# One PSUM tile for each bank of the two MoE stages, and the state product on all four quarters of TensorE

## Chip, cores and metric

One core of a Trainium2 chip runs the whole program. The metric is the device time of one execution in microseconds, the median of three runs: 1067.89 us for the kernel before (1065.71 to 1068.6).

## The reference

Gated linear attention is followed by two mixture layers without routing ("moe" and "moe2"), all in float32. The sizes are 4 batches x 8 heads x 768 positions x 48 per head, 3072 tokens of 384, and hidden widths of 1536 and 768.

```
f = sigmoid(f_logit)
for t in range(768):
    state = f[:, :, t, :, None] * state + outer(k[:, :, t], v[:, :, t])
    y[:, :, t] = q[:, :, t] @ state
x = y as (3072, 384)
x = ((x @ w_a) * (x @ w_b)) @ w_out
out = max(x @ w1, x @ w2, x @ w3) @ w_out2
```

## The kernel before

**Segments.** The tokens are cut into 12 segments of 256, three to a batch. A segment goes through attention and then through the first moe; its result is stored to a scratch in DRAM. When all 12 are done, the second moe runs over 6 blocks of 512 tokens.

**Attention of a segment** (`attn_steps`, line 384; `direct_steps`, 311, or `near_steps`, 218, ahead of it). Products inside groups of 8 positions are made on VectorE and GpSimd. TensorE turns the decayed k, q and the partial result (`p_tr`, `p_od`), then makes the products between positions (`p_sc`, 491, and `p_av`, 508, with the masks of line 505 between them) and carries the state: `p_u` (452) makes the new part of the state of each of four chunks of 64 positions, `decay` (462) and `gain` (466) add it up in `st`, and `p_in` (479) multiplies the state that a chunk begins with by that chunk's decayed q, which line 547 puts into `kt`. Heads lie in eight places: `hl`, the half of the 128 partitions (0 to 63 or 64 to 127), and `hi` from 0 to 3. `p_in` issues 64 products of 48 x 48 by 48 x 64 in a segment (48 where the state is still zero). It reads partitions `64 * hl` and writes PSUM partitions `64 * hl`. `p_av` reads the half `hl ^ hp` and writes the half `hl`, with both values of `hp` next to each other.

**First moe of a segment** (`moe1_steps`, 571). Numbers are split into a high and a low part, so each product is three matmuls in place of one. For each pair jj of the 12 tiles of hidden width: `up` a twice (9 matmuls of 256 columns each, line 591), a copy `c_a` on ScalarE out of PSUM (597), `up` b twice, `v_ab` on VectorE (601) that multiplies a by the b in PSUM, `c_g` on ScalarE (605) and `v_g` on VectorE (610) that split the product, and two `y` (9 matmuls each, 619) that add onto the three sums of the result. `c_y` (625, 627) copies the finished sums out.

**Second moe.** `up2` (777) writes tiles of one bank each, from the pool `ps_p` of four buffers, which ScalarE (787) and VectorE (789) read; `down` (804) adds onto four sums of 384 columns, which `c_down` (811) copies out.

**PSUM.** The pool `ps_m` holds one tile of four banks, made once (line 138), and everything of the two moes but `up2` lives in it: a in bank 0, b in bank 1, the sums of `y` in banks 2 and 3, and the four sums of `down` in banks 0 to 3. The conversion of the first three weight groups on TensorE (`s5p`, 698, and one copy of 3 x 384 columns, `s5c`, 706) uses banks 0 to 2. The other four banks are attention's (`ps_o`, `ps_w`) and later `up2`'s.

```
bank = ps_m.tile([P, 4, 2 * SEG], F32, name="bank")
pair = [bank[:, i].rearrange("p (a x) -> p a x", a=2) for i in range(4)]
ps2[w] = pair["ab".index(w)]           # up
yps[0], yps[1] = pair[2], pair[3][:, 0] # y
o_ps[t] = bank[:, t, 0:DM]             # down
```

**Order.** Every piece of work is a step with a letter for its kind (`step`, 146). `ORDER` is a string written out ahead of time: its letters say which kind's next step is issued, so it sets the order in which each engine's instructions, and the DMAs of SyncE's queue, are queued; the semaphores between engines are placed by the tile framework from what each instruction reads and writes. `flex` steps (150) may run on VectorE or GpSimd; `ON_POOL` lists the numbers of those that run on GpSimd.

Of the kernel before, what the change touches and what calls it, by code (L numbers as in the profile page):

```python
# [19 lines left out]
    "zzzqkjillvtrdrcrzrdrdTUddrTdrUdrddrdTdUrdr0dPdPrdkb1brg20PrPqhgq31gr2b5jbg3grgghbggr0hrgPhrhb1r6Thrb"  # L20
    "52Vrrcd3rTdT0rVrdTr61Pr25hrrh3hkhh6Phv4h0tPhP01P2h31P4Tlbl2Uxb0ddxdTdUd13d2TssUe4s3ed0edm4md0m1d2mnd"
    "PP3m1jbbfgmg2nmg3hgmfcg4Pnybgfg0gyhgdmgv4mbn1mbhm2PPbf3ThdybnhVm4mdThTyVhTdfPrdnrrmrhfrmrhndthmdhfmd"
    "hn0hmdPfhdn10Pd2yhy13PdP2cyh43yPdmlb4cmxfbnmdfxmdnmddyfsdkydneqjPPbfmbgdyhgdPgybdgdcmgdbmngdbnmnhYgd"
    "mgdfhmnmfhmnghyfgdyndmfmdyndvydmdmdPfPndmbhmbPfhnmtdhdhyhydhdmhdhPfdhndPfmhdydPcdPdcyhdPdmlbmxnddmdx"
    "PPfbdmbjnmhqkgdsmmfcdyendygfdPnmgdbgfmbdbygdgydhgdmnngnmYhmfnhmfmgnhdmygfvdnmfmdmdnmdPfPdmbhbmPdmhtd"
    "mhdhyhdhynhPdhfPdndyhfydnPfPdyhdcydcdPmlbdbmxddmndxPPdbgmbjmhqkgfgsPgdnmbgemcdbmfbdnygfyhndyfdmgdgyd"
    "gdhymndnmYnhmdmhvmfdnmfmgnddyfdnPPfybdbydPhdytmdmdhmndhmdhmdfmdnfmdnhcydhcdyhdhPdhPddmkhdmfqjdnPPfmh"
    "ydncdPylbddbdmxddPPbdxmbgdmhfgPdnmbgvfmsgdnybgebygdmghmfggnhmgmfhydhPdPybhbmnnnYPdfhmtdhnmfhdmnyhdhd"
    "hyhPdhdPdmhdPfPdnmdcfchmdyndPdylbdmxdddPPbgkmbgxgggmhfgndPqjmbhsmfbeynbgdygchmmfgdnmhfmhngdydydmddmf"
    "dnmfmdndyvdydmdPfPndmbfmbdhPdytyhdmhnndhnmYhmdhfhnPdhdPfmhdyndydccdPdPmhdPdmlbddkdqbmxPPfbdmbjxnmghd"  # L30
    "gfPdnmbgdysgfdbygcdgmbenhmgdmgdfmgndyfghynmdmhvfmhnydydmdmfdnPfPdmbhbyndPhdythdmhdhmhdhmhdPhdfndPfmh"
    "dydccdydPnndPnYdmhkmddPfqdjnmlbmbfxdmnmxcdmfdnmdPsPfdmbnbemdPgfdmbdbhmgbdmgdmdvyydydnyfgndPfgmdnmfmg"
    "ndhmgdmfmdgmdmgdhyyghPdnhybdbyfhdnPfmtndmfcdhmcdhhdmhdyydydkhydhqdhjPnnnYhdfPnmhdcPfPdmhdmnddmdddmfn"
    "mdmfvdnPmlbddmxfdPPbgxybdgmdghdmsmgdgdygePdnPbfybdnybhmdfggmgdngyfdnmhcmdhmcfhmddmmdydPnkdydbfbjyqhd"
    "nyfmdnmcfmdmddPdyhtdhdyhdhydhPndnnYfmdvnmfmhndmhdmfdnmfmdnmdmfdmmdmdddPyhdydydnfPdnPdfmdhmdmmPylbbyx"
    "nfynxyfnmfmsmnemyfynfyyyPPnbmdcbgdmgnghYPnggPdbgdmcbmbghmdfnmfmgndyghymdghdPmbhdbmfhnPfmthndyhhydhhm"
    "dhhdPhdfnPfmdhydydPPmhPnmlbbmxPPfbgxmbgggnmghgfPhPnbyggsgygbebmhmhPfmbhhnmbPfmhnhhyhhhyhhPPmhmfnmfmy"
    "ymnnnYPfmnfmmnmmfnmfmnmmfmmmyyynfPnyhfmnmfmnmmfmmmPybyxynxfynyfnyfsywWeWyWWmWnWnWmWWmWnmWAWmfWmnBpAf"
    "mCyWDyBWCnmWEDmfWnmWfAmWEWyWynBGYCmGAmHfmHGBmDHCmpnufDEunfnEAmfyyGBAHyCyNuGBDMCGuEDuMAEHuNHNBpMuCMDM"
    "uNENuMMuMummnmmfnmfmnoyyWWmWufnfoyAyunBnYCoooNoNMoDMoMoEoNoNouMoMooouuMNMuNoMooouuMGGHNHGMuNHpuMuMNM"  # L40
    "uNuMoMoOuOXuXuuooOoOXoNoNMoMuMXNNMuMuMuuuoooooNoNMoMuMuuGGHGHHoopNoNMoMoMooNoNMouoMoOoOXoOuOXuMNMuXN"
    "uMXuMNMuNuMuMuuuoooooNoNMoMuMuuooNoNMoMuMuuGGHGHHoopNoNMoMoMooNoNMouoMoOoOXoOuOXuMNMuXNoMoXoouuMNMuN"
    "oMooouuMNMuNuMuMNMuNuMuMuuoGoGHoGHoHoNoNMoMoMooNoMouoNoOoOXoOuOXuMuXMNMuNXoMooouuMNMuNoMooouuMNMuNoM"
    "ooouuMNMuNoMooouuMNMuNoMooouuMNMuNoMoOoOXoOuOXuMNMuXNuMXoMoNouMuNuMuMuuuooNoNMoMuMuuooNoNMoMuMuooNoN"
# [952 lines left out]
```

## Time and profile before

| what | value |
|---|---|
| median of three runs | 1067.89 us |
| the profiled execution, its own time | 1064.77 us |
| its span, first to last instruction | 1063.0 us |
| mean granted TensorE clock | 0.990 of full speed |
| first matmul of the first moe | 60 us |
| first matmul of the second moe | 726.6 us |
| last `up` of the first moe | 762 us |

The span is what the trace shows; 1.8 us lie around it. The trace has three parts: the start with loads and conversions of weights and the attention of segment 0 (to 60 us), the 12 segments of the first moe with the other segments' attention between them (60 to some 762 us, the second moe's first products among the last of them), and the second moe. TensorE is the engine that is busy throughout, so the reading goes by what ends its idle times. A matmul's row is longer than the distance to the next one, since matmuls are pipelined: distances between starts tell the pace, durations do not.

### The profile page before, as it was taken

The page shows a single profiled execution, that of the slowest core. Times are in us where ns is not written, and L with a number is a line of the kernel's source. Part 1 is how long each engine was busy: PE and PEld are TensorE (multiplying, and loading weights), DVE is VectorE, ACT ScalarE, POOL GpSimd, SP SyncE. Part 2 cuts the span into 40 slices and gives each one's busy share as a digit, 9 for nine tenths or more (in the row PEclk, how much of TensorE's full clock was granted, in tenths as well). Part 3 has the DMA queues.
Part 4 walks back from the last instruction along what each step waited for, and adds up shares of the span by engine and source line. Part 5 has one row for each costly group of instructions (what it writes and reads, how often), then busy time and mean ns, then how long its engine had stood idle before and what let it go on. Part 6 is the DMA issues. An engine that isn't in the chain of part 4 may idle for free.

```text
span 1063.0 us, 23346 instructions
## 1 busy us (share of the span) xinstructions
PE 944.6 (89%) x10367; PEld 851.2 (80%) x10367; DVE 508.2 (48%) x714; ACT 330.3 (31%) x504; POOL 324.5 (31%) x299
## 2 busy tenths in 40 slices
...
DMA packets 31973, 72.93 MB, mean 69 GB/s; under 512 B 4224, under 2 KB 13184, under 8 KB 31872
## 3 DMA queue, kind: packets, MB, share of 16 engines
...
## 4 chain that ended last, share of the span: by engine, by line
PE 80%; DVE 7%; ACT 6%; issue 2%; DMA 1%; SPq 0%; DVEq 0%; ACTq 0%
PE bank L591 29%; PE p L777 21%; PE bank L619 15%; PE bank L804 7%; DVE a L601 4%; ACT a L597 3%; PE o L517 1%; PE o L487 1%; PE w L500 1%; PE w L397 1%; DVE gl L610 1%; PE w L459 1%; PE o L397 1%; ACT ub L811 1%; DMA xf<-xf 1%
## 5 line engine op out<-in xcount | busy, mean ns | idle before, releaser
L591 PE MATMUL bank<-xh,ua 128*128 128x256 f32 x864 | 169.2, 293 | 34.6 <-DVE a L601 29.5
L619 PE MATMUL bank<-gh,uo 128*128 128x256 f32 x864 | 165.5, 290 | 22.3 <-ACT a L597 14.4
L591 PE MATMUL bank<-xh,ub 128*128 128x256 f32 x864 | 165.1, 288 | 20.6 <-ACT a L597 17.6
L591 PEld LDWEIGHTS bank<-xh,ua 128*128 128x128 f32 x864 | 135.5, 193 | 45.3 <-DVE a L601 38.4
L777 PE MATMUL p<-ub,u 128*128 128x512 f32 x486 | 165.5, 395 | 0.0
L619 PEld LDWEIGHTS bank<-gh,uo 128*128 128x128 f32 x864 | 134.3, 192 | 30.4 <-ACT a L597 19.0
L591 PEld LDWEIGHTS bank<-xh,ub 128*128 128x128 f32 x864 | 134.2, 192 | 27.4 <-ACT a L597 22.5
L601 DVE TENSOR_TENSOR a<-a,bank 128x512 f32<-128x512 f32 x72 | 49.5, 687 | 200.9 <-PE bank L591 153.5
L591 PE MATMUL bank<-xl,ua 128*128 128x256 f32 x432 | 123.1, 285 | 0.6 <-DVE xl L582 0.6
L619 PE MATMUL bank<-gl,uo 128*128 128x256 f32 x432 | 122.6, 284 | 0.1
L591 PE MATMUL bank<-xl,ub 128*128 128x256 f32 x432 | 121.9, 282 | 0.0
L605 ACT CAST gh<-a 128x512 fp32r<-128x512 f32 x72 | 44.7, 620 | 218.0 <-DVE a L601 169.8
L777 PEld LDWEIGHTS p<-ub,u 128*128 128x128 f32 x486 | 90.7, 187 | 20.5
L789 DVE TENSOR_TENSOR ua<-ua,p 128x512 f32<-128x512 f32 x72 | 49.4, 686 | 112.5 <-PE p L777 111.8
L777 PE MATMUL p<-ua,u 128*128 128x512 f32 x324 | 101.7, 395 | 0.0
L610 DVE TENSOR_TENSOR gl<-a,gh 128x512 fp32r<-128x512 f32 x72 | 61.0, 847 | 51.9 <-ACT gh L605 51.7
L591 PEld LDWEIGHTS bank<-xl,ua 128*128 128x128 f32 x432 | 83.5, 193 | 0.9 <-DVE xl L582 0.9
L619 PEld LDWEIGHTS bank<-gl,uo 128*128 128x128 f32 x432 | 83.0, 192 | 0.3 <-DVE gl L610 0.3
L597 ACT COPY a<-bank 128x512 f32<-128x512 f32 x72 | 42.3, 587 | 131.6 <-PE bank L591 92.9
L591 PEld LDWEIGHTS bank<-xl,ub 128*128 128x128 f32 x432 | 82.7, 191 | 0.0
L777 PEld LDWEIGHTS p<-ua,u 128*128 128x128 f32 x324 | 60.6, 187 | 13.8
L793 ACT CAST uo<-ua 128x512 fp32r<-128x512 f32 x36 | 22.3, 620 | 150.4 <-DVE ua L789 88.1
...
## 6 DMA issues: line engine op xcount, KB each, us to landing
...
```

Source lines behind the costliest of these rows:

```text
L397: mm(pair[0][h], lhsT=pair[1][h], rhs=ident[half(h), half(h)], is_transpose=True, start=first_of_bank(n), stop=True, skip_group_check=True)
L459: mm(ws["u"][half(hl), par, g, hi], lhsT=k64n[ps, g, hi, half(hl)], rhs=vst[ps, g, hl ^ (hi // 2), hi], start=True, stop=True, skip_group_ ...
L591: mm(ps, lhsT=col(w, i, j, h), rhs=x2[x][:, i], start=(n == 0), stop=(n == 3 * KC - 1), skip_group_check=True)
L597: act.copy(out=g2[jj][0], in_=ps2["a"])
L601: vec.tensor_mul(out=a, in0=a, in1=ps2["b"])
L605: act.copy(out=g2[jj][1], in_=g2[jj][0])
L610: vec.tensor_sub(out=g2[jj][2], in0=a, in1=gh.bitcast(F32))
L619: mm(ps, lhsT=wts["o", j // 3][:, j % 3, w, m * P:m * P + P], rhs=g, start=(j == j0 and n == 0 and m != 1), stop=(j == j1 - 1 and n == 2), ...
L777: mm(ps, lhsT=col(n, i, f, w), rhs=y[:, i], start=(c == 0), stop=(c == 3 * KC - 1))
L789: vec.tensor_max(out=hset[k][0], in0=hset[k][0], in1=u_ps[b, f, n])
L793: act.copy(out=hh, in_=h)
L804: mm(o_ps[t], lhsT=h[:, t * P:t * P + P], rhs=wts["q", f // 3][:, f % 3, w], start=(f == 0 and n == 0), stop=(f == NF - 1 and n == 2))
```

## The change

- The tile of four banks is gone. Each use asks the pool for a tile of one bank by name: `pa` and `pb` for `up`, `y01` and `y2` for `y`, the four in turn for `down`, and `pa`, `pb`, `y01` for `s5p`, which is now three steps, each with its own copy `s5c` of 384 columns.
- For the heads with `hi` of 2 and 3 the state lies in the other half of the partitions: `p_u` writes it there, line 547's product of q is made by three instructions (one for `hi` 0 and 1 on all partitions, two for `hi` 2 and 3, each reading one half of the partitions and writing the other), and so is `tot`, the decay over a chunk (line 422). `p_in` then reads the half `hl ^ (hi // 2)`, and its loop goes over `hi` in the order 0, 2, 1, 3.
- `ORDER` and `ON_POOL` are new as a whole: 2583 steps in place of 2523 (48 from the split products, 12 from `s5p` and `s5c`), 639 of them flex in place of 591. Which steps there are is otherwise the same.

```diff
--- before.py
+++ after.py
@@ -17,51 +17,52 @@
 
 
 ORDER = (
...
 )
 
 
 ON_POOL = {
...
 }
 
 NEAR = 2
@@ -135,8 +136,8 @@
     ps_o = at_stack.enter_context(tc.tile_pool(name="ps_o", bufs=1, space=bass.MemoryType.PSUM))
     ps_w = at_stack.enter_context(tc.tile_pool(name="ps_w", bufs=1, space=bass.MemoryType.PSUM))
 
-    bank = ps_m.tile([P, 4, 2 * SEG], F32, name="bank")
-    pair = [bank[:, i].rearrange("p (a x) -> p a x", a=2) for i in range(4)]
+    def bank(tag):
+        return ps_m.tile([P, 2 * SEG], F32, tag=tag, name=tag)
 
     raw = {}
     wts = {}
@@ -376,6 +377,8 @@
         flex("d", lambda e: e.tensor_add(out=opv[:, :, 4:8, 0:D], in0=opv[:, :, 4:8, 0:D],
                                    in1=pv[:, :, 0, :].rearrange("p (h t) d -> p h t d", h=2)))
 
+    CROSS = ((slice(0, 2), slice(0, P), slice(0, P)), (slice(2, 4), slice(0, 64), slice(64, P)),
+             (slice(2, 4), slice(64, P), slice(0, 64)))
     xf = {}
     KL = [k8.rearrange("p x r -> p (x r)"), k16.rearrange("p x l r -> p (x l r)"), k32.rearrange("p x l r -> p (x l r)")]
     q8 = qt.rearrange("p (x two) r -> p two x r", two=2)[:, 1]
@@ -419,7 +422,10 @@
             flex("g", lambda e: e.tensor_mul(out=a4, in0=fv[:, :, :, 3], in1=tv[:, :, :, 3]))
             flex("g", lambda e: e.tensor_mul(out=gt[:, :, 4:8], in0=gt[:, :, 0:4], in1=_bc(a4[:, :, 1], 2, 4)))
             flex("g", lambda e: e.tensor_mul(out=ft[:, :, 4:8], in0=ft[:, :, 8:12], in1=_bc(a4[:, :, 0], 2, 4)))
-            flex("g", lambda e: e.tensor_mul(out=tot.rearrange("p a b -> p (a b)"), in0=a4[:, :, 0], in1=a4[:, :, 1]))
+            a4v = a4.rearrange("p (a b) i -> p a b i", a=4)
+            for a, dst, src in CROSS:
+                flex("g", lambda e, a=a, dst=dst, src=src: e.tensor_mul(
+                    out=tot[dst, a], in0=a4v[src, a, :, 0], in1=a4v[src, a, :, 1]))
 
         def p_tr(src):
             w = ws["x"] = banks(ps_w, "w")
@@ -456,7 +462,7 @@
                     for par in range(2):
                         for hl in range(2):
                             ps = half(par)
-                            mm(ws["u"][half(hl), par, g, hi], lhsT=k64n[ps, g, hi, half(hl)],
+                            mm(ws["u"][half(hl ^ (hi // 2)), par, g, hi], lhsT=k64n[ps, g, hi, half(hl)],
                                rhs=vst[ps, g, hl ^ (hi // 2), hi], start=True, stop=True, skip_group_check=True)
 
         def decay(c, e):
@@ -481,12 +487,13 @@
             for c in range(4):
                 if first and c == 0:
                     continue
-                for hi in range(4):
+                for hi in (0, 2, 1, 3):
                     o = (hi % 2) * SEG + 64 * c
                     for hl in range(2):
+                        r0 = 64 * (hl ^ (hi // 2))
                         mm(os_[0][64 * hl:64 * hl + D, hi // 2, o:o + 64],
-                           lhsT=st[64 * hl:64 * hl + D, c, hi * D:hi * D + D],
-                           rhs=qv[64 * hl:64 * hl + D, hi, c], start=False, stop=True, skip_group_check=True)
+                           lhsT=st[r0:r0 + D, c, hi * D:hi * D + D],
+                           rhs=qv[r0:r0 + D, hi, c], start=False, stop=True, skip_group_check=True)
 
         def p_sc(g):
             w = ws["s", g] = banks(ps_w, "w").rearrange("p h (i x) -> p h i x", i=2)
@@ -544,7 +551,10 @@
         step("b", lambda: act.copy(out=q16[:, :, 0, :], in_=sib(qt)[:, :, 1, 0, :]))
         flex("h", lambda e: e.tensor_mul(out=q16[:, :, 1, :], in0=sib(qt)[:, :, 1, 1, :], in1=_bc(tsib[:, :, 2], 2, 8)))
         flex("h", lambda e: e.tensor_mul(out=q32, in0=hc(qt)[:, :, 4:8, :], in1=_bc(ft[:, :, 8:12], 3, 8)))
-        flex("h", lambda e: e.tensor_mul(out=hc(kt), in0=hc(qt), in1=_bc(ft[:, :, 0:8], 3, 8)))
+        for a, dst, src in CROSS:
+            y = slice(4 * a.start, 4 * a.stop)
+            flex("h", lambda e, y=y, dst=dst, src=src: e.tensor_mul(
+                out=hc(kt)[dst, y], in0=hc(qt)[src, y], in1=_bc(ft[src, y, 0:8], 3, 8)))
         if late:
             late(os_)
         step("P", p_u)
@@ -583,7 +593,7 @@
 
         def up(w, j):
             if j % 2 == 0:
-                ps2[w] = pair["ab".index(w)]
+                ps2[w] = bank("p" + w).rearrange("p (a x) -> p a x", a=2)
             ps = ps2[w][:, j % 2]
             n = 0
             for i in range(KC):
@@ -611,7 +621,8 @@
 
         def y(j, j0, j1):
             if j == j0:
-                yps[0], yps[1] = pair[2], pair[3][:, 0]
+                yps[0] = bank("y01").rearrange("p (a x) -> p a x", a=2)
+                yps[1] = bank("y2")[:, 0:SEG]
             gh, gl = (g[:, j % 2] for g in g2[j // 2][1:])
             for m in range(KC):
                 ps = yps[0][:, m] if m < 2 else yps[1]
@@ -695,17 +706,14 @@
             w = wts[groups[n]]
             e.tensor_sub(out=w[:, :, 1], in0=t, in1=w[:, :, 0].bitcast(F32))
 
-        def s5p(n):
+        def s5p(n, i):
             t = live[n][1].bitcast(F32).rearrange("p (i c) -> p i c", i=3)
-            w = wts[groups[n]]
-            for i in range(3):
-                mm(bank[:, i, 0:DM], lhsT=ident, rhs=t[:, i], start=True, stop=False, skip_group_check=True)
-            for i in range(3):
-                mm(bank[:, i, 0:DM], lhsT=minus, rhs=w[:, i, 0], start=False, stop=True, skip_group_check=True)
-
-        def s5c(n):
-            live.pop(n)
-            act.copy(out=wts[groups[n]][:, :, 1], in_=bank[:, 0:3, 0:DM])
+            ps = live[n, i] = bank(("pa", "pb", "y01")[i])[:, 0:DM]
+            mm(ps, lhsT=ident, rhs=t[:, i], start=True, stop=False)
+            mm(ps, lhsT=minus, rhs=wts[groups[n]][:, i, 0], start=False, stop=True)
+
+        def s5c(n, i):
+            act.copy(out=wts[groups[n]][:, i, 1], in_=live[n, i])
 
         for n in range(len(groups)):
             step(kinds[0], s1, n)
@@ -713,8 +721,9 @@
             flex(kinds[2], lambda e, n=n: s3(n, e))
             step(kinds[3], s4, n)
             if n < on_pe:
-                step(kinds[5], s5p, n)
-                step(kinds[6], s5c, n)
+                for i in range(3):
+                    step(kinds[5], s5p, n, i)
+                    step(kinds[6], s5c, n, i)
             else:
                 flex(kinds[4], lambda e, n=n: s5(n, e))
 
@@ -799,7 +808,7 @@
     def down(b, f, t):
         _, hh, hl = hset[(b * NF + f) % 2]
         if f == 0:
-            o_ps[t] = bank[:, t, 0:DM]
+            o_ps[t] = bank(("pa", "pb", "y01", "y2")[t])[:, 0:DM]
         for n, (h, w) in enumerate(((hh, 0), (hh, 1), (hl, 0))):
             mm(o_ps[t], lhsT=h[:, t * P:t * P + P], rhs=wts["q", f // 3][:, f % 3, w], start=(f == 0 and n == 0), stop=(f == NF - 1 and n == 2))
 
```

## Rows read from the trace of the kernel before

**Rows 1.** The page, part 1: busy time, share of the span, instructions of each engine.

```profile
PE 944.6 (89%) x10367; PEld 851.2 (80%) x10367; DVE 508.2 (48%) x714; ACT 330.3 (31%) x504; POOL 324.5 (31%) x299
```

**Rows 2.** Waits of PE: waited for, us in total, times, longest us.

```profile
PE bank L591 <- DVE a L601: 30.3, 39, 1.3
PE bank L591 <- ACT a L597: 19.7, 28, 1.4
PE bank L619 <- ACT a L597: 14.4, 21, 0.8
PE bank L619 <- DVE a L601: 7.6, 9, 0.9
PE bank L804 <- ACT ub L811: 6.8, 12, 0.6
PE bank L591 <- ACT ysb L627: 3.2, 3, 1.3
```

**Rows 3.** Timeline, 653 to 659 us: start us, us, engine, what, [idle before].

```profile
653.68 0.28 PE L591 MATMUL bank<-xl,ua 128*128 128x256 f32 x1
654.76 0.28 PE L591 MATMUL bank<-xl,ub 128*128 128x256 f32 x1
655.07 0.58 ACT L597 COPY a<-bank 128x512 f32<-128x512 f32 x1 [2.93 <-PE bank L591]
655.71 0.50 PE L591 MATMUL bank<-xh,ub 128*128 128x256 f32 x2 [0.68 <-ACT a L597]
...
658.98 0.50 PE L591 MATMUL bank<-xh,ua 128*128 128x256 f32 x2 [0.85 <-DVE a L601]
```

**Rows 4.** Chain in order of time, 640 to 690 us: start us, us, what.

```profile
646.15 2.16 PE bank L619 x18
...
655.71 2.43 PE bank L591 x18
...
658.98 2.42 PE bank L591 x18
...
662.06 2.43 PE bank L591 x18
```

**Rows 5.** Groups by form: count, busy us, mean ns, idle before and what ended it.

```profile
L777 PE MATMUL p<-ub,u 128*128 128x512 f32 x486 | 165.5, 395 | 0.0
...
L610 DVE TENSOR_TENSOR gl<-a,gh 128x512 fp32r<-128x512 f32 x72 | 61.0, 847 | 51.9 <-ACT gh L605 51.7
...
L601 DVE TENSOR_TENSOR a<-a,bank 128x512 f32<-128x512 f32 x72 | 49.5, 687 | 200.9 <-PE bank L591 153.5 <-PE bank L619 33.9 <-ACT a L597 13.5
...
L605 ACT CAST gh<-a 128x512 fp32r<-128x512 f32 x72 | 44.7, 620 | 218.0 <-DVE a L601 169.8 <-PE bank L619 48.3
...
L811 ACT COPY ub<-bank 128x384 f32<-128x384 f32 x24 | 10.9, 480 | 35.3 <-PE bank L804 35.3
```

**Rows 6.** Timeline of PE, one p_in and one p_av of a segment.

```profile
477.47 1.94 PE L487 MATMUL o<-kt,st 48*48 48x64 f32 x62
...
481.35 0.89 PE L517 MATMUL o<-ab,vlev 64*48 64x64 f32 x48
```

**Rows 7.** Groups by form: products into kt (1024 columns) and k32 (512).

```profile
L547 POOL TENSOR_TENSOR kt<-qt,ft 128x1024 f32<-128x1024 f32 x8 | 18.3, 2285 | 20.5 <-PE w L397 16.5 <-DVE a L601 3.9
...
L540 DVE TENSOR_TENSOR k<-kt,gt 128x512 f32<-128x512 f32 x8 | 5.8, 724 | 0.1
...
L547 DVE TENSOR_TENSOR kt<-qt,ft 128x1024 f32<-128x1024 f32 x4 | 5.7, 1424 | 0.0
...
L540 POOL TENSOR_TENSOR k<-kt,gt 128x512 f32<-128x512 f32 x4 | 5.6, 1392 | 0.2
```

**Rows 8.** Stretches: length, busy us of PE, PEld, DVE, ACT, POOL; clock.

```profile
80.00:140.00 60.00, 50.44 (x868) 46.56 (x866) 44.41 (x58) 23.40 (x33) 31.47 (x24) 1.00 0.26 89
140.00:560.00 420.00, 375.19 (x5326) 352.51 (x5326) 245.24 (x356) 116.73 (x196) 215.34 (x202) 1.00 0.18 58
```

**Rows 9.** Line 708: duration ns min/median/max, start.

```profile
L708 ACT CAST ua<-bank x1: 1141/1141/1141, 28.5 to 28.5; 128x1152 fp32r<-128x1152 f32 x1
```

More of the change, by code (lines that the diff above doesn't have):

```diff
@@ L19 @@
 ORDER = (
[L20 to L44, printed above, removed]
@@ L45 @@
-    "MoMoMooNoMoooOoOXoOOXXX"
+    "zzzqkjtivllrdrcdrzrdrTrUdddrTdUdrddTrdUdrdPdPbr0gdjkggb1vg02PrPhrggh3gr1gbr52b5rg6gb5gr3gh6r505rhhPr"
+    "hbr61Tbkh65Vcq26T0qTrhrV63r1T2rPr5h5rh6h3h5hrd6P0hrdr4hdPt610h2PP13h4PTlblU2xb0ddxdTd3d1Ud4sTssUded0"
+    "ededm2PPb13mgdb2jmnPmbd3gmvhgfc4Pbmng4bm0fmgdygnd0yghgfmgghnmgfPgnhydbhyb1hT1mhVhm2TThf32dmnVmf3T4Pn"
+    "rrryrdrhm4rtyhdmhd0mfhdhmhdnP10hm2Pf3dynh4yP1Pdmh2cmPd3fdmlbdmc4xbnmfdxnyfdyndkfPPbdybgdjggqgsyhePng"
+    "dnmbYgdmcghbmgdngbdmhmfgdmnghmghfmdndyfdndyfmdydvdydmdPnPdmbhbmdhdPhfmtnhfmhdynhdhyhdhmhPdhdPdmhdmfc"
@@ new lines @@
+    "dnPdcfPdyhyddPkdmdlbdqmnxPPbdmbxgdmgdPjhmbfdnmgdbsmfbgceyngdyfgghmndfmdgdyyhmndnnmYhvghmfdmnfmdngdyg"
+    "dygdPdPdmhbbdmfhPndhmtfmhndhydhyhdhdmhdhPfPdncmfchdydPdPyhdPdkdmlbdqbmxnPPbdmbxgmfhjgndPmbfgsdyngdyb"
+    "gecmbgdgmhgdmfghnmmghmfhnygfgydnddmmfdyydvmndnnmYdmdfnPdPmbfbmdnyhdhyhPdmthdhmdfnmhdfmhdnyhdyhdhcPdh"
+    "PdcdmhdmfndPPfkdmhdyndjqydPdmlbddcmxbdPPfbgxmbdgdngmhdgfPdmnsybebyggbghmghmfnmhfmgnhydygdvmmfggdnmfm"
+    "ddydydPnPndnYmhbmhbfndPhmtdmfhndyhdyhmdhhmdfmdhnhcPdfcmhdndydmddkdPfqjdynmfmhdyndcdyddPPdmhdddPmlbdm"
@@ new lines @@
+    "xfdnmfxPdnmbdyvgdysgdPmbemfghnPdPgdbgmbfbmdnygdhydggdmhmfgmhnghPfmbhbydhyghdPndnngYmdhcthcmdhdfmnhmd"
+    "hmdhkdhPdfPqjdnyyhdmfcPdndPfmhdydndydddPdmlbbvdmxPPfbgmbdxgdnmgdPhPbgdmsmfbbdnyedygmfdnmgdfmdnydygdh"
+    "mgmdgmfdnhmcdmfcPgngygdbfdynbPfhytdhydhmkndndmYhdjmnqhmdmfcmhndmfdnmhdyhfdmnhdmfhmndhdmhdhPfPdmhvdmd"
+    "PdPdmhdPdmlbdbyxddPPnbxydbfyhngPfgPbdgygdnbmfsgdmbemngdgcdmhcmgfmghmgdghmgdhPybdbyhnPfhnytfdmnhkfmhd"
+    "mhdmhdqjyhdyyhdyhchdhPnnndPYfmhnmfdydnmddPdPmhdmfvdmnmfdnmddmfdmdmdmdPdylbdyxdndyfdnxPybfgdnmgdfmdsg"
@@ new lines @@
+    "dmnemgdmfgmggggmgggmyynfynyfnyfPydbdcyhkhPnPndbYdmjcbmqbdmnhmdcPfhmbdhnmdbhPdfmtdnyhdyhmdhhmdfhnmhfm"
+    "hndyhvdyhdPdPdmhmfdnPfPdyhdyPdmlbdbmxdndPPbdxmbgdmhfdPngPgcdsmfcbgmengydbgdbyhmdmgdfmgndghmgfPhnmbdh"
+    "ybgfyghndPhmtfdmyhdyhdmhndnhndhmYhmdhdmfhndhPdPfdnmhydydPdPmhPfnmlbfmbxynyxPPbgmbggggmgshgPhPbgmebgb"
+    "mfghnmgfmgnhyfhnyfmyymmnPmhbbmhfnPhfmhhyhnhyhhmhhmmfnmfmymyPnnnPYfmhnmfmnmmfnmfPnPmhPmbmxfmxmyysynew"
+    "WyWfWnyWWWyWWmWWmfWAmWmWnBmWAfCWyWynWBDmfWmCnWmfDWEmnWEyAmfmnBAfyCyDByCmnnnmYEDmfnmpfAmEyynBACmmfnBm"
```

6 lines of the change are left out of this document (added), and 31 rows, old and new, of the table ON_POOL.

## The prediction

> **What bounds the kernel now.** I read the page first: TensorE is busy 944.6 us of the span of 1063.0 us [rows 1], VectorE, the next, 508. So TensorE sets the end, and the question is what makes up the other 118 us and what makes its busy time long.
>
> The waits of PE come next [rows 2]. Six of them concern the tile `bank` of the two moes: 30.3 + 19.7 + 14.4 + 7.6 + 6.8 + 3.2 = 82.0 us in 39 + 28 + 21 + 9 + 12 + 3 = 112 waits, some 0.7 us each. That is the length of one copy or product out of PSUM, so each time TensorE stands still while one such operation runs.
>
> Are these waits the data's? The line names say no. L619 (`y`, banks 2 and 3) waits 21 times for L597, which reads bank 0 alone. The timeline shows one case whole [rows 3]. The last product into bank 0 starts at 653.68 and ends at 653.96. The copy out of bank 0 could go then; it starts at 655.07, just after the product into bank 1 that began at 654.76 has ended. The next product, again into bank 1, waits for the copy and starts at 655.71. Both waits are between different banks of one tile: whoever touches the tile waits for the last other engine that did, in the order of the string. The counter-example is in the same trace: L777 writes tiles of one bank each, which ScalarE and VectorE empty, and has 0.0 us of idle time before 486 matmuls [rows 5].
>
> The trace also bears on a rule that would leave the change nothing to gain. The Trainium skill, "Perfetto Trace Analysis", section Matmuls, says that independent groups should rotate through different PSUM banks so that emptying one overlaps the next group's matmuls. By that rule the kernel before, whose a and b rotate, would lose nothing here, and the change would bring only what `p_in` saves; this trace does not agree, with its 82.0 us.
>
> **The change part by part.**
>
> *One tile per bank.* Each wait costs more than its idle time, because the pipeline drains and fills. The chain shows it [rows 4]: 18 matmuls in an unbroken run take 2.16 us (0.12 each), but from 655.71 to 658.98 there are 3.27 us for 18 that end in a wait for L601, and from 658.98 to 662.06 3.08 us for 18 that end in one for L597. The loss is 1.11 and 0.92 us, 0.25 more than the idle time that the timeline gives such waits (0.85 and 0.68 [rows 3]). So 112 waits cost 82.0 + 112 x 0.25 = 110.0 us. All lie on the path, since TensorE is what ends last. That includes the twelve of L804 behind `c_down`.
>
> What is late next, once they are gone? `up` of b must wait until `v_ab` has read the last b: 0.69 us [rows 5]. In the new order at least two groups of nine matmuls (2.16 us) stand between, attention aside. The first `y` of a pair needs `v_ab`, `c_g` and `v_g`: 0.69 + 0.62 + 0.85 = 2.16 us. In 60 of 72 pairs three or more groups (3.24 us) stand between, in the others attention's products fill up. So no true wait is forced by the order alone. What can bring some back is that VectorE and ScalarE work in order: an attention product of 1.42 us [rows 7] ahead of `v_ab` uses up the slack of 2.16 us. 1.42 + 0.69 and the 0.25 us of the pipeline make 2.36, so such a case costs 0.2 us. I take one in seven of the 216 places in the first moe (72 pairs, each with an `up` a, an `up` b and a `y` that may wait), 30, at 0.2 us: 6 us. Then, from 80 to 140 us, VectorE is busy 44.4 of 60 us with weights and attention, and TensorE idles 9.6 us [rows 8]; TensorE cannot run away from its inputs there, and I leave 6 us of that in place. The other ends are 0 and, if half of the 110.0 us come back, 55.
>
> *The state product on four quarters.* `p_in` starts 62 matmuls in 1.94 us, less 0.22 for the last one's own length: 1.72 / 61 = 28.2 ns each. `p_av`, whose neighbours use four different pairs of input and output halves, starts 48 in 0.89: 0.67 / 47 = 14.3 ns [rows 6]. After the change four neighbours of `p_in` also differ. For 704 matmuls that is 704 x (28.2 - 14.3) ns = 9.8 us, all of it on TensorE's path. Ends: 0 if quarters do not overlap here, 9.8 by the nearest row. I take 9.8, since input height, output width and loop are nearly those of `p_av`.
>
> *What pays for it.* Line 547's one product of 1024 columns (GpSimd 2.29 us, VectorE 1.42) becomes three of 512, by L540 1.39 and 0.72 us each [rows 7]: 4.17 and 2.16 us, so 1.9 or 0.7 us more in a segment. No row shows half the partitions; the length of a row goes with the columns in those I have, so I take no saving from them (the lower end would be half, about nothing extra). The two further products for `tot` have 4 or 8 columns and cost less than 0.72 each. Over 12 segments that is 15 to 40 us spread on two engines that are free for 175 and 205 of the 420 us from 140 to 560 us [rows 8]. On the path: 0. If that cover is gone, `p_in` waits for `kt`, at most 1.9 + 1.4 = 3.3 us a segment.
>
> *Conversion of three groups.* One copy of 1152 columns (1.14 us [rows 9]) becomes three of 384 (0.48 each in L811's row [rows 5]): +0.3 us for each of three groups on ScalarE, against the first copy no longer waiting for the other two banks. Between -1 and +1 us; I take 0.
>
> *The order.* The same DMAs are issued on SyncE's queue, moved by a few places at the start; the first 20 us of loads keep their sequence but for v_tok and v of segment 0, which go ahead of two larger loads. 0, with 3 us either way.
>
> **Sum.** Against the profiled execution's own 1064.8 us: 1064.8 - 110.0 - 9.8 + 12 = 957.0 us. The median of the runs stands 3.1 us above that execution, so the forecast is **960 us**. A measurement of this kernel can tell about 0.3% (3 us) from no change.
>
> **The rivals.**
>
> *True waits take the place of the false ones.* VectorE and GpSimd together have 461 us of work in the 420 us from 140 to 560 us [rows 8]. When TensorE runs ahead by a tenth, the in-order queues delay `v_ab` and `v_g` behind attention's products. For it: `a` has a single buffer, so `c_a` of the next pair waits for `v_g` of this one. Against: VectorE waited 187 us for TensorE before its 72 `v_ab` [rows 5], so it was early, not late. With half of the 110.0 us back: 1064.8 - 55 - 9.8 + 3.1 = 1003 us, from 985 to 1020.
>
> *The change does not do what it says.* If a wait belongs to the chip's banks or to the pool rather than to the tile, only `p_in` pays: 1064.8 - 9.8 + 3.1 = 1058 us. For it: all of these engines do share one PSUM. Against: L777's row [rows 5]. The rule of the Trainium skill's "Perfetto Trace Analysis", section Matmuls, named above, comes to the same time, since the banks rotate already.
>
> *Slower: the attention chain becomes the bound.* The place is line 547 with `tot`, `decay` and `gain` ahead of `p_in`. A segment takes some 56 us now ((726.6 - 60) / 12); if its attention needs that time anyway, by chains between VectorE and GpSimd, TensorE's gain turns into waiting, and the 3.3 us of extra products lengthen each segment: 1067.9 + 12 x 3.3 = 1107 us. It decides from the point where attention cannot be done faster than 56 us a segment. Against it: both engines are free for over 40% of the stretch, and PE's waits in rows 2 are for the moe's readings.
>
> **How the numbers follow.** Forecast 0.77, with its own range 938 to 980 (0 to 20 us of waits left, the start's 3 us, another few us for the run); true waits 0.15; no effect of the tiles 0.05; slower 0.03. The range that leaves 2 in 10 out is 938 to 1006: the forecast's bulk and half of the first rival. Faster by over 0.3%: the first three cases, less a little for the third, 0.95. Within 0.3%: 0.02. Slower: 0.03.
>
> **What would show it.** Right: no wait of L591, L619 or L804 for a reader of another bank, and these lines' idle time under 20 us; L597 starting when the last `up` of a ends; `p_in` of 64 matmuls in about 1.1 us; 18 matmuls every 2.16 us through the moe. Wrong: long waits of PE for L601, L597 or L610 that the data demand (first rival); the 112 waits unchanged (second); PE waiting for L463, L471 or L547 ahead of `p_in` (third).

## The result, and the profile after

The changed kernel takes 953.3 us (median of 4 runs, 953.13 to 953.37), the kernel before 1068.0 on the same chip: a ratio of 0.8929, interval 0.8914 to 0.8945. The forecast was 960 us, the range 938 to 1006. Lines have moved: `up` is now L601 (was L591), `y` L630 (L619), `down` L813 (L804), `c_a` L607 (L597), `v_ab` L611 (L601), `c_g` L615 (L605), `v_g` L620 (L610), `p_in` L494 (L487), the product into `kt` L556 (L547).

Part 1 of the page of the changed kernel (engine, busy us, share of the span, instructions), beside [rows 1]; PE is TensorE, PEld its loading of weights, DVE VectorE, ACT ScalarE, POOL GpSimd:

```profile
PE 909.3 (96%) x10367; PEld 837.8 (88%) x10367; DVE 544.0 (57%) x753; ACT 331.5 (35%) x510; POOL 314.4 (33%) x308
```

The span is 951.4 us, 111.6 less. TensorE's idle time fell from 118.4 to 42.1 us. Its busy time fell too, by 35.3 us for the same 10367 matmuls: 9.7 of that is `p_in`; the other 25.6 us are near the 28 us that the prediction has for the pipeline's draining and filling, 0.25 us at each of 112 stops.

The waits of PE in the moe, changed kernel (waited for, us in total, times, longest us), beside [rows 2]:

```profile
PE y L630 <- DVE gl L620: 3.6, 6, 0.9
...
PE y L630 <- ACT gh L615: 2.6, 3, 1.4
...
PE pb L601 <- POOL ub L707: 0.4, 1, 0.4
...
PE pb L601 <- DVE a L611: 0.3, 1, 0.3
```

Of the 112 waits none is left. The 11 that remain are true ones: `y` needs g, `up` of b needs its weights, or needs `v_ab` to have read that very bank.

The timeline of the changed kernel, 175 to 176 us (start us, us, engine, what), shows what [rows 3] did not allow. Bank a's copy runs from 175.63 to 176.23, and TensorE writes into bank b all through it, a matmul every 0.12 us:

```profile
175.40 0.40 PE L601 MATMUL pb<-xh,ub 128*128 128x256 f32 x2
...
175.63 0.60 ACT L607 COPY a<-pa 128x512 f32<-128x512 f32 x1
175.64 0.28 PE L601 MATMUL pb<-xl,ub 128*128 128x256 f32 x1
...
175.76 0.40 PE L601 MATMUL pb<-xh,ub 128*128 128x256 f32 x2
```

The chain in order of time of the changed kernel, 600 to 630 us (start us, us, what), beside [rows 4]: TensorE alone, and each piece starts where the one before it ends.

```profile
600.90 2.16 PE pb L601 x18
603.06 1.08 PE y L630 x9
604.14 2.16 PE pa L601 x18
```

`p_in` of 64 matmuls, timeline of PE in the changed kernel, beside [rows 6]; its 704 matmuls are busy 12.4 us, 22.1 before:

```profile
285.48 1.11 PE L494 MATMUL o<-kt,st 48*48 48x64 f32 x64
```

Where did the 111.6 us come from? The first `up` starts at 61.0 us (60.0 before), the first matmul of the second moe at 632.1 (726.6). The stretch between shrank by 95.5 us and the second moe by 17.1 (336.4 to 319.3), less 1.0 at the start. In the second moe there is no attention. The tiles alone (experiment one) shorten that part to 322.6 us, which is 13.8 of the 17.1 us. The other 3.2 us are the order's: from the first matmul of the second moe to the end stand 1521 matmuls in place of 1548, so 27 of the first moe, at 0.12 us each, have moved to the stretch before it.

One thing did not go as told. Stretches of the changed kernel (length, busy us of PE, PEld, DVE, ACT, POOL with their counts; granted clock, DMA share, GB/s):

```profile
80.00:140.00 60.00, 57.01 (x997) 54.27 (x996) 53.72 (x66) 25.26 (x36) 30.93 (x26) 1.00 0.27 92
140.00:160.00 20.00, 17.00 (x343) 15.73 (x342) 16.56 (x23) 3.44 (x6) 8.31 (x9) 0.91 0.10 25
160.00:400.00 240.00, 236.98 (x3511) 227.63 (x3511) 182.97 (x254) 81.84 (x138) 146.72 (x145) 1.00 0.23 75
```

TensorE still stands idle 9.0 us between 80 and 400 us (3.0 in each of the three stretches); after that it is nearly gapless. VectorE is busy 53.7 of 60 us and 16.6 of 20 in the first two stretches. Whether that is the price of the exchanged halves is what several of the experiments ask.

### The profile page after: what moved, and what is told of

Its sections match the earlier page's. It is cut to its first block, busy times and chain, and to the rows that moved or that the text cites. A ratio compares the mean times of both kernels' runs of the same rounds, so it can differ in the third digit from the quotient of the medians.

```text
span 951.4 us, 23429 instructions
## 1 busy us (share of the span) xinstructions
PE 909.3 (96%) x10367; PEld 837.8 (88%) x10367; DVE 544.0 (57%) x753; ACT 331.5 (35%) x510; POOL 314.4 (33%) x308
## 4 chain that ended last, share of the span: by engine, by line
PE 77%; DVE 9%; DMA 5%; POOL 4%; issue 2%; ACT 1%; SPq 1%; DVEq 0%; POOLq 0%; ACTq 0%
PE p L786 24%; PE y L630 13%; PE pb L601 12%; PE pa L601 12%; PE y L813 4%; PE pb L813 2%; PE pa L813 2%; PE o L524 2%; DMA fn<-in_f_logit_dram 2%; PE w L400 2%; DMA ub<-in_moe_w_b_dram 1%; PE w L507 1%; DVE gl L620 1%; DMA uo<-in_moe_w_out_dram 1%; PE w L465 1%
## 5 line engine op out<-in xcount | busy, mean ns | idle before, releaser
L601 PE MATMUL pb<-xh,ub 128*128 128x256 f32 x864 | 164.7, 288 | 0.7 <-POOL ub L707 0.4
L630 PE MATMUL y<-gh,uo 128*128 128x256 f32 x864 | 161.6, 286 | 2.6 <-ACT gh L615 2.6
L601 PE MATMUL pa<-xh,ua 128*128 128x256 f32 x864 | 163.2, 288 | 0.0
L630 PEld LDWEIGHTS y<-gh,uo 128*128 128x128 f32 x864 | 134.9, 192 | 4.5 <-ACT gh L615 3.2
L601 PEld LDWEIGHTS pb<-xh,ub 128*128 128x128 f32 x864 | 134.9, 192 | 3.6 <-POOL ub L707 0.6
L601 PEld LDWEIGHTS pa<-xh,ua 128*128 128x128 f32 x864 | 134.9, 192 | 2.2
L630 PE MATMUL y<-gl,uo 128*128 128x256 f32 x432 | 123.3, 285 | 3.6 <-DVE gl L620 3.6
L601 PE MATMUL pa<-xl,ua 128*128 128x256 f32 x432 | 122.4, 283 | 0.0
L601 PE MATMUL pb<-xl,ub 128*128 128x256 f32 x432 | 122.4, 283 | 0.0
L615 ACT CAST gh<-a 128x512 fp32r<-128x512 f32 x72 | 44.6, 619 | 124.5 <-DVE a L611 115.6
L630 PEld LDWEIGHTS y<-gl,uo 128*128 128x128 f32 x432 | 83.1, 192 | 5.1 <-DVE gl L620 5.1
L611 DVE TENSOR_TENSOR a<-a,pb 128x512 f32<-128x512 f32 x72 | 49.2, 684 | 66.2 <-PE pb L601 43.3
L601 PEld LDWEIGHTS pa<-xl,ua 128*128 128x128 f32 x432 | 83.1, 192 | 0.0
L601 PEld LDWEIGHTS pb<-xl,ub 128*128 128x128 f32 x432 | 83.1, 192 | 0.0
L620 DVE TENSOR_TENSOR gl<-a,gh 128x512 fp32r<-128x512 f32 x72 | 62.5, 869 | 27.1 <-ACT gh L615 26.4
```

The costliest lines, as they stand in the source:

```text
L601: mm(ps, lhsT=col(w, i, j, h), rhs=x2[x][:, i], start=(n == 0), stop=(n == 3 * KC - 1), skip_group_check=True)
L611: vec.tensor_mul(out=a, in0=a, in1=ps2["b"])
L615: act.copy(out=g2[jj][1], in_=g2[jj][0])
L620: vec.tensor_sub(out=g2[jj][2], in0=a, in1=gh.bitcast(F32))
L630: mm(ps, lhsT=wts["o", j // 3][:, j % 3, w, m * P:m * P + P], rhs=g, start=(j == j0 and n == 0 and m != 1), stop=(j == j1 - 1 and n == 2), ...
```

## The experiments

They are called e1 to e12 in this order. Every kernel is timed against the kernel before on the same chip. That kernel's median was 1066.7 us beside the first four, then 1065.4 (e5 to e8), 1066.7 (e9 to e11) and 1066.2 (e12). Where kernels of different chips are compared, the ratios are.

**One: the tiles alone.** The kernel before with one tile per bank; order and halves as they were.

```diff
-    bank = ps_m.tile([P, 4, 2 * SEG], F32, name="bank")
-    pair = [bank[:, i].rearrange("p (a x) -> p a x", a=2) for i in range(4)]
+    def bank(tag):
+        return ps_m.tile([P, 2 * SEG], F32, tag=tag, name=tag)
...
-                ps2[w] = pair["ab".index(w)]
+                ps2[w] = bank("p" + w).rearrange("p (a x) -> p a x", a=2)
...
-            o_ps[t] = bank[:, t, 0:DM]
+            o_ps[t] = bank(("pa", "pb", "y01", "y2")[t])[:, 0:DM]
```

> The kernel before with one PSUM tile per bank and nothing else: old order, old p_in, s5p and s5c each still one step (s5c as three copies). Theory (the 112 waits belong to the tile, and the old order forces no true ones): the waits of PE for L597, L601, L811 and L625 sink from 82 us to under 15, and the time is 1068 - 110 + about 12 = 970 us (960 to 985). Rival (the new order makes the gain; without it true waits take their place): above 1010 us.

956.3 us, 0.8964 (0.8935 to 0.8993): 110.4 us less. The waits of PE in this kernel for a reader of PSUM or for g (the moe's inputs aside):

```profile
PE y L620 <- DVE gl L610: 1.8, 2, 1.6
...
PE pa L591 <- ACT a L597: 0.4, 1, 0.4
```

The tiles bring all of the 110 us by themselves, without the new order. That is below the expected 960 to 985 us: true waits of the moe come to 2.2 us, not to the 12 that the prediction set aside.

**Two: the halves alone.** The kernel before with the exchange; `tot` and `kt` are each made in three products, in one step of the order.

```diff
...
-                for hi in range(4):
+                for hi in (0, 2, 1, 3):
...
+                        r0 = 64 * (hl ^ (hi // 2))
...
-                           lhsT=st[64 * hl:64 * hl + D, c, hi * D:hi * D + D],
-                           rhs=qv[64 * hl:64 * hl + D, hi, c], start=False, stop=True, skip_group_check=True)
+                           lhsT=st[r0:r0 + D, c, hi * D:hi * D + D],
+                           rhs=qv[r0:r0 + D, hi, c], start=False, stop=True, skip_group_check=True)
...
-        flex("h", lambda e: e.tensor_mul(out=hc(kt), in0=hc(qt), in1=_bc(ft[:, :, 0:8], 3, 8)))
+        flex("h", lambda e: [e.tensor_mul(out=hc(kt)[dst, 4 * a.start:4 * a.stop], in0=hc(qt)[src, 4 * a.start:4 * a.stop],
+                                          in1=_bc(ft[src, 4 * a.start:4 * a.stop, 0:8], 3, 8)) for a, dst, src in CROSS])
```

> The kernel before with the exchanged halves of the state and nothing else (one tile of four banks, old order; the split products are issued one after the other inside the old steps, on the engine that the step had). Theory (p_in lies on TensorE's path, the added products do not): 1068 - 9.8 = 1058 us, p_in of 64 matmuls in about 1.1 us in place of 2.0. Rival (the products of 512 columns and of tot delay p_in, or p_in was hidden): 1066 to 1072 us.

1060.7 us, 0.9951 (0.9926 to 0.9976): 6 us less. Its `p_in` is busy 12.7 us, so the 9.4 us are there; the waits of PE show the bank waits untouched and one that has grown (it was `PE w L500 <- DVE st L471: 0.5, 1, 0.5` before):

```profile
PE bank L597 <- DVE a L607: 31.0, 40, 1.3
PE bank L597 <- ACT a L603: 19.4, 27, 1.4
...
PE w L505 <- DVE st L475: 3.3, 4, 1.1
```

`p_sc`, just behind `p_in` on TensorE, writes the tile `w` that the last `gain` reads. I take it that the longer `p_in` had covered that read; no run separates this from a `gain` that comes later. The 2.8 us more, with 0.25 us of restart for each of three more waits, make 3.6 us, about what is missing from the 9.4.

**Three: both, in the old order.** The edits of the first two experiments together.

```diff
-    bank = ps_m.tile([P, 4, 2 * SEG], F32, name="bank")
...
+    def bank(tag):
+        return ps_m.tile([P, 2 * SEG], F32, tag=tag, name=tag)
...
+                        r0 = 64 * (hl ^ (hi // 2))
...
```

> Both of these edits in the old order, so that what is left to the changed kernel is the order and the split of s5p. Theory (the parts add up): 960 us (950 to 975), e1 less about 9.8. Rival (the new order is needed to use what the tiles free): above 985 us.

956.7 us, 0.897 (0.8944 to 0.8997): the same as the tiles alone, not 9.8 us less as the expectation had it. With the bank waits gone, the halves bring nothing in this order; the wait of `p_sc` has grown:

```profile
PE w L505 <- DVE st L475: 5.6, 6, 2.1
```

The changed kernel, with 0.8929, is some 3 to 4 us below this one. That is what the new order is worth, together with the split of `s5p` and the engines chosen for the split products, at the edge of what can be told. What brings it is open: the wait of `p_sc` falls from 5.6 to 1.0 us in the changed kernel, but the waits of `y` and `up` for readers, g or weights rise from 0.5 to 6.9 us; and from 60 to 80 us TensorE is busy 18.64 us at a granted clock of 0.78 here, 19.84 us at 0.91 in the changed kernel.

**Four: the new order and the halves, with one tile.** The changed kernel with the four banks in one tile again.

```diff
+    one = ps_m.tile([P, 4, 2 * SEG], F32, name="bank")
+
     def bank(tag):
-        return ps_m.tile([P, 2 * SEG], F32, tag=tag, name=tag)
+        return one[:, ("pa", "pb", "y01", "y2").index(tag)]
...
```

> The changed kernel with the four banks in one tile again, all else as it is (new order, exchanged halves). Theory: the waits come back, some 110 us of them: 1050 to 1080 us. Rival (the order, not the tiles, carries the gain): under 1000 us.

1075.6 us, 1.0084 (1.0057 to 1.0112): 0.8% slower than the kernel before, and 122 us above the changed one. The largest waits of PE in this kernel:

```profile
PE bank L603 <- DVE a L613: 34.0, 44, 1.2
PE bank L632 <- ACT a L609: 24.8, 37, 0.9
PE bank L603 <- ACT a L609: 16.2, 20, 1.4
...
PE bank L632 <- DVE a L613: 7.1, 9, 0.9
PE bank L815 <- ACT ub L822: 5.5, 9, 0.9
```

These are 87.6 us in 119 waits; seven more for `ysb`, `ua` and `uo` bring it to 91.8 us in 126. With 0.25 us of restart each, 91.8 + 31.5 = 123 us: the prediction's way of pricing them gives the measured 122. The new order is no cure for the waits of one tile; it has more of them.

**Five: two tiles of two banks.** The first experiment's kernel with banks 0 and 1 in one tile, 2 and 3 in another.

```diff
-    def bank(tag):
-        return ps_m.tile([P, 2 * SEG], F32, tag=tag, name=tag)
+    bank_ab = ps_m.tile([P, 2, 2 * SEG], F32, name="bank_ab")
+    bank_y = ps_m.tile([P, 2, 2 * SEG], F32, name="bank_y")
+    bank = lambda i: (bank_ab, bank_y)[i // 2][:, i % 2]
...
```

> The kernel before with two tiles of two banks: a and b share one, the sums of y the other (s5c as three copies). Theory (a wait is for the last other engine on the same tile): the waits of L619 for L597 and L601 (14.4 + 7.6 us) and of L591 for L625 (3.2) go, 33 waits with 0.25 us each besides; a and b still wait for each other: 1068 - 33 = 1035 us (1028 to 1045). Rival (a wait that y no longer has comes at the next product into a or b): above 1055 us.

1012.5 us, 0.9498 (0.9482 to 0.9514): 53 us less, and below the expected 1028 to 1045 us. The waits of PE that are left for another bank's reader:

```profile
PE bank_ab L593 <- DVE a L603: 25.3, 33, 0.9
PE bank_ab L593 <- ACT a L599: 15.1, 23, 0.7
```

The expectation had counted only `y`'s waits and those for `ysb`. All twelve of `down` for its copy went too, and the waits inside the tile of a and b shrank from 50.0 us [rows 2] to 40.4. So 41.6 us of waiting in 56 waits are gone; with 0.25 us each that is 41.6 + 14.0 = 56 us, near the 53 measured. I read the shrinking as the other half of the rule in [rows 3]: a reader also waits for later writes into its tile, and with `y` in another tile it starts earlier. No run separates that half. Both tiles are made once here, while experiment one asks the pool anew at each use; that half of the gain comes without asking anew says that the division counts. Four tiles made once were not run.

**Six: the halves undone.** The changed kernel with `p_in` on two quarters, `tot` and `kt` in one product each.

```diff
...
-                            mm(ws["u"][half(hl ^ (hi // 2)), par, g, hi], lhsT=k64n[ps, g, hi, half(hl)],
+                            mm(ws["u"][half(hl), par, g, hi], lhsT=k64n[ps, g, hi, half(hl)],
...
-                for hi in (0, 2, 1, 3):
+                for hi in range(4):
...
-                        r0 = 64 * (hl ^ (hi // 2))
+                        r0 = 64 * hl
...
-            flex("h", lambda e, y=y, dst=dst, src=src: e.tensor_mul(
-                out=hc(kt)[dst, y], in0=hc(qt)[src, y], in1=_bc(ft[src, y, 0:8], 3, 8)))
+            flex("h", lambda e, y=y: y.start or e.tensor_mul(
+                out=hc(kt), in0=hc(qt), in1=_bc(ft[:, :, 0:8], 3, 8)))
```

> The changed kernel with the state's halves not exchanged: p_in on two quarters, one product for kt and one for tot (the two steps each that this leaves over issue nothing). Theory: 953.3 + 9.8 = 963 us, p_in of 64 in about 2.0 us. Rival (the exchange costs elsewhere what p_in saves): 951 to 956 us.

955.6 us, 0.8968 (0.8954 to 0.8981), where the prediction's own term says 963. `p_in` is back at its old length in the timeline of this kernel:

```profile
282.77 1.99 PE L494 MATMUL o<-kt,st 48*48 48x64 f32 x64
```

So 9.7 us of TensorE's work come back and the kernel loses 2 us by the medians, 4 by the ratios. So something in the exchange gives back 5 to 7 us.

**Seven: the order of the quarters.** The changed kernel with heads in order, so that of four neighbours two are often on the same pair of halves.

```diff
-                for hi in (0, 2, 1, 3):
+                for hi in range(4):
```

> The changed kernel with p_in's loop over hi in the order 0, 1, 2, 3: two neighbours on one pair of quarters, then two on the other. Theory that a product starts, in order, as soon as its own quarter is free: 0 waits, 1 and 2 go together, 3 and the next 0 go together, so p_in keeps some 14 ns a matmul and the time stays within 1 us of 953.3. Rival that only four neighbours on four different quarters overlap: 28 ns a matmul, 963 us.

954.2 us, 0.8955 (0.8941 to 0.8968), which can't be told from the changed kernel's. `p_in` of 64 in the timeline of this kernel, and its group by form (busy us, mean ns of one):

```profile
285.12 1.15 PE L494 MATMUL o<-kt,st 48*48 48x64 f32 x64
```

```profile
L494 PE MATMUL o<-kt,st 48*48 48x64 f32 x704 | 12.9, 219 | 0.0
```

Of eight matmuls the first four here use two quarters in turn, the last four the other two. That costs 0.5 us against four different neighbours, where two quarters throughout cost 9.7 (e6). So what counts here is that each quarter gets two of eight. The expectation's account, that a matmul starts in order as soon as its own quarter is free, fits the 1.15 us; no run tells it from one in which a waiting matmul lets the next one pass.

**Eight: the exchange's products left out.** The changed kernel without the two products of 64 partitions that write the crossed half of `kt`. It leaves out the decayed q of half of the heads.

```diff
-            flex("h", lambda e, y=y, dst=dst, src=src: e.tensor_mul(
+            flex("h", lambda e, y=y, dst=dst, src=src: y.start or e.tensor_mul(
```

> The changed kernel without the two products of 64 partitions into kt (heads of hi 2 and 3 are left out there, so the output is not the reference's). Theory (they lie beside TensorE's work): 953.3 within 1 us. Rival (they lie on the path to p_in or delay v_ab in VectorE's and GpSimd's queues): 950 us or less.

945.9 us, 0.8875 (0.8862 to 0.8888): 7 us less than the changed kernel by the medians, 6 by the ratios. The stretches of this kernel, to be held against those of the changed one:

```profile
80.00:140.00 60.00, 57.87 (x1006) 55.19 (x1005) 53.24 (x67) 26.18 (x37) 27.38 (x24) 1.00 0.27 92
140.00:160.00 20.00, 18.55 (x379) 17.20 (x378) 16.13 (x24) 5.76 (x9) 7.54 (x9) 1.00 0.25 86
160.00:400.00 240.00, 239.59 (x3531) 231.02 (x3530) 179.92 (x259) 84.06 (x141) 135.39 (x140) 1.00 0.22 70
```

TensorE's busy time rises by 0.86, 1.55 and 2.61 us, 5.0 in all, of the 9.0 that it stood idle in the changed kernel. The rest of the 6.4 us between the two spans fits the granted clock, 0.91 from 140 to 160 us in the changed kernel's profile and 1.00 here. The three waits of `y` for `c_g` (2.6 us) are gone too: `y` here waits only for `gl`, 2.7 us. The groups of the product into `kt` in the changed kernel, by form (busy us, mean ns of one, idle before); the two of 64 partitions are those left out here:

```profile
L556 POOL TENSOR_TENSOR kt<-qt,ft 64x512 f32<-64x512 f32 x17 | 22.0, 1293 | 3.5 <-ACT a L607 1.6 <-PE w L400 0.8
L556 DVE TENSOR_TENSOR kt<-qt,ft 64x512 f32<-64x512 f32 x7 | 8.4, 1206 | 0.2
...
L556 DVE TENSOR_TENSOR kt<-qt,ft 128x512 f32<-128x512 f32 x6 | 7.9, 1318 | 0.0
L556 POOL TENSOR_TENSOR kt<-qt,ft 128x512 f32<-128x512 f32 x6 | 6.5, 1084 | 27.4 <-PE w L400 23.8 <-DVE prod L342 3.6
```

They are 24 products and 30.4 us. That their absence gives TensorE 5 us is shown. How they reach it can be followed at the longest wait of `y`, 1.39 us. From the timeline of the changed kernel, 136 to 145 us, in the columns used above:

```profile
136.91 3.34 POOL L556 TENSOR_TENSOR kt<-qt,ft 64x512 f32<-64x512 f32 x2
...
137.74 1.57 DVE L556 TENSOR_TENSOR kt<-qt,ft 128x512 f32<-128x512 f32 x1
...
139.24 1.42 DVE L325 TENSOR_TENSOR prod<-qn,kn 128x384 f32<-128x384 f32 x1
...
141.97 0.68 DVE L611 TENSOR_TENSOR a<-a,pb 128x512 f32<-128x512 f32 x1
...
143.35 0.50 PE L630 MATMUL y<-gh,uo 128*128 128x256 f32 x2 [1.39 <-ACT gh L615]
```

From the timeline of this kernel, 135.5 to 144.5 us:

```profile
137.79 0.68 DVE L556 TENSOR_TENSOR kt<-qt,ft 128x512 f32<-128x512 f32 x1
...
138.39 0.55 DVE L325 TENSOR_TENSOR prod<-qn,kn 128x384 f32<-128x384 f32 x1
...
140.24 0.68 DVE L611 TENSOR_TENSOR a<-a,pb 128x512 f32<-128x512 f32 x1
```

VectorE has the same five operations in both, from L324 (136.86 and 136.60 us) to `v_ab` (L611); none of the products left out stands among them. But in the changed kernel two of these run on GpSimd at that time, where GpSimd is idle from 137.05 to 139.07 us in this one. Beside them VectorE's own product into `kt` takes 1.57 us in place of 0.68 and the next one 1.42 in place of 0.55, so `v_ab` comes 1.5 us later, and `c_g` and `y` with it. So one way is that GpSimd's products lengthen VectorE's. The other, a product that stands in VectorE's own queue, is there too (64x512, 0.69 us, at 82.71 us). How the 5 us divide between the two is not shown.

**Nine: the exchange by DMA.** One product of 128 partitions writes the crossed half to a tile `kx`, and two DMAs of SyncE carry it over.

```diff
+    kx = at.tile([P, 64, 8], F32, name="kx")
...
         def gain(c):
+            if c == 1:
+                for a, dst, src in CROSS[1:]:
+                    sp.dma_start(out=kt[dst, 64:128], in_=kx[src])
...
+        for n, to in enumerate((hc(kt)[:, 0:8], hc(kx), None)):
+            y = slice(8 * n, 8 * n + 8)
+            flex("h", lambda e, y=y, to=to: to is not None and e.tensor_mul(
+                out=to, in0=hc(qt)[:, y], in1=_bc(ft[:, y, 0:8], 3, 8)))
```

> The changed kernel with the exchange taken off VectorE and GpSimd: line 556's product goes by two instructions of 128 partitions (the second into a tile of its own), and two DMAs of 128 KB on SyncE's queue, issued ahead of the second gain, bring its halves to their places. Theory (the 7 us between the changed kernel and e8 are the third instruction and the slow halves in the two in-order queues): one instruction of 512 columns more than e8, none less than before: 947 to 950 us, with fewer waits of PE for L615 and L620. Rival (p_in waits for the DMAs, or SyncE's queue holds the loads behind them): 955 us or more.

956.6 us, 0.8971 (0.8954 to 0.8988): a miss, 3.5 us above the changed kernel on the same chip. The waits of PE in this kernel say why:

```profile
PE o L498 <- DMA kt<-kx: 6.2, 2, 3.5
```

Both waits are in the first two segments, where the copies are issued just behind loads of weights on SyncE's queue. From 160 to 400 us TensorE is busy 239.20 us, 2.2 more than in the changed kernel.

**Ten: the exchange by ScalarE.** As nine, with `act.copy` in the DMA's place.

```diff
+                for a, dst, src in CROSS[1:]:
+                    act.copy(out=kt[dst, 64:128], in_=kx[src])
...
```

> The same with two copies on ScalarE (64 partitions x 512 columns) in place of the two DMAs. Theory: ScalarE is busy 35%, but works in order, so a copy of some 0.6 us ahead of c_a or c_g costs a little: 948 to 953 us. Rival (ScalarE's queue waits for GpSimd's product and holds c_a behind it): 955 us or more.

950.7 us, 0.8909 (0.8893 to 0.8925), with the 24 copies by form in this kernel:

```profile
L476 ACT COPY kt<-kx 64x512 f32<-64x512 f32 x24 | 14.8, 619 | 0.8 <-DVE kx L560 0.4
```

**Eleven: the changed kernel again**, on the chip of nine and ten.

> The changed kernel as it is, on the same chip as the two others, for comparison: 953 us, within 2.

953.1 us, 0.8934 (0.892 to 0.8948). In this profile the clock is 1.00 from 140 to 160 us and TensorE's busy time there again 17.00 us: the idle time belongs to the kernel, while the clock does not fall in every execution. Ten is 2.4 us below it, and the intervals of the ratios touch.

**Twelve: the DMA from segment 2 on.** Nine's exchange, with the changed kernel's own in segments 0 and 1.

```diff
         def gain(c):
-            if c == 1:
+            if s >= NEAR and c == 1:
                 for a, dst, src in CROSS[1:]:
                     sp.dma_start(out=kt[dst, 64:128], in_=kx[src])
...
```

> The exchange by DMA of e9 from segment 2 on alone; segments 0 and 1 as in the changed kernel, since in e9 p_in waited 6.2 us there for the DMAs, which stood in SyncE's queue behind loads of weights. Theory (between the start and the second moe e9 was some 2 to 4 us shorter than the changed kernel): 947 to 951 us, and no wait of p_in for a DMA. Rival (the DMAs cost elsewhere what they save): 952 us or more.

948.2 us, 0.8897 (0.8878 to 0.8916): the lowest of the complete kernels, 5 us below the changed one by the medians and 3 to 4 by the ratios. The view of DMA issues of this kernel (issues, KB each, median us from issue to landing), and below it a stretch in the columns used above:

```profile
kt<-kx SPq DMA_DIRECT2D x20, 128.0 KB, 4.2
```

```profile
160.00:400.00 240.00, 239.99 (x3552) 231.89 (x3553) 182.28 (x259) 85.05 (x143) 143.81 (x145) 1.00 0.25 78
```

From 160 to 400 us TensorE is without a gap, busy 3.0 us more than in the changed kernel. The start, whose two segments are the changed kernel's, is left to gain.

## Why the prediction was right, and where its steps were off

**The waits belong to the tile.** Right. One tile per bank alone brings 110.4 us where the step said 110.0; two tiles bring half; putting the one tile back costs 122. The price of 0.25 us for the restart beside each wait holds within 3 us in three kernels: 56 against 53 us, 123 against 122, 110.0 against 110.4. The rival that the tiles do nothing (1058 us) is refuted by e1 and e4. The rule of the Trainium skill ("Perfetto Trace Analysis", section Matmuls) that rotating banks let the emptying overlap does hold here once each bank is a tile of its own: in the timeline after, the copy of a (175.63 to 176.23 us) and the matmuls of b run side by side.

**The 12 us that come back.** Too much. I had set aside 6 us for in-order queues and left 6 of 9.6 idle us from 80 to 140 us in place. The tiles alone gave back 2.2 us of moe waits (the changed kernel has 6.9, and 3.5 without the crossed products, e8), and from 80 to 140 us TensorE idles 3.0 us in the changed kernel. TensorE could run faster there than I had thought, while VectorE went from 44.4 to 53.7 busy us. With it the first rival (1003 us) falls: `y` and `up` wait 6.9 us in all. Its mechanism is visible, but off TensorE's path: `c_a` waits 38.3 us for `v_g` because `a` has a single buffer, and hardly any of it arrives at TensorE.

**`p_in`.** The term itself was sized right: 9.8 us predicted, 9.7 measured by the groups, at 14 ns a matmul. What it brings to the end is 6 us beside the bank waits (e2), nothing in the old order without them (e3), and 2 to 4 us in the changed kernel (e6).

**What pays for it: "On the path: 0".** This is the step that failed. The extra work was within the 15 to 40 us that I gave: the 36 products into `kt` take 22.0 + 8.4 + 6.5 + 7.9 = 44.8 us, where 12 took 24.0 [rows 7], and the 24 small ones for `tot` on 64 partitions 11.6 us. The end I kept out, that half of the partitions take less time, was rightly kept out. But I costed VectorE's at 0.72 us each, and they took 1.2 to 1.3: 0.68 is the time with GpSimd idle, and in the changed kernel each of the 13 has a GpSimd instruction beside it for part or all of its time, and nine take 1.0 us or more. And I argued from the average freedom of the two engines from 140 to 560 us [rows 8]. An average says neither what stands ahead of `v_ab` in VectorE's queue nor what GpSimd does to it meanwhile. Of the 5.0 us, 2.4 lie between 80 and 160 us, where VectorE is busy 70.3 of 80 us in the changed kernel, the other 2.6 up to 400 us; so a full VectorE alone does not account for them. Leaving out the 24 products of 64 partitions brings 6 to 7 us (e8); moving the crossing to ScalarE or, from segment 2 on, to the DMA brings 2 to 5 (e10, e12). The slower rival (1107 us) named this place and its 3.3 us a segment. Its extra products did cost time, 6 to 7 us in the whole run and not 3.3 us in each of 12 segments; attention never became the bound.

**The order.** 0 with 3 us either way: some 3 to 4 us of gain (e3 against the changed kernel), at the upper end or just past it; its cause is open.

**The conversion.** 0, with 1 us either way. The first `up` starts at 60.0 us before, 62.0 with the tiles alone, 61.0 and 60.1 in two executions of the changed kernel; no run separates the term.

**The sum.** Against 957.0 us for a profiled execution stand the 953.4 us of this one. The errors nearly cancel, and that is luck. Along the runs the tiles bring 110.4 us, where 98.0 stood after the 12 set aside; the halves bring nothing in the old order and 2 to 4 us in the changed kernel, where 9.8 stood; and the order 3 to 4 us, where 0 stood. The tiles, which are nearly all of the gain, were priced rightly.
